# A fused attention and expert kernel: two product evictions made one, the second batch's scores moved by 8 steps, four stores halved

## The chip, the cores and the metric

The kernel runs on one core of a Trainium2 chip. The time is the device time of one execution in microseconds (us); lower is better. The engines are named as in the profile: PE (TensorE's matmuls, PEld its weight loads), DVE (VectorE), ACT (ScalarE), POOL (GpSimd), SP (SyncE). Here POOL and SP mostly issue DMAs.

## What is computed

```
for each of 4 batches (q, k, v: 6080 x 256, float32):
    qn, kn = q, k with each column divided by (its norm over the 6080 rows + 1e-6)
    s  = kn^T @ qn / tau              # 256 x 256, the "scores"
    a  = softmax of s over its last axis
    x  = v @ a                        # 6080 x 256
over all 24320 rows of x:
    h  = x @ w_in                     # 256 -> 2048
    g  = s * relu(h)^2 + b
    out = g @ w_out                   # 2048 -> 256, float32
```

## The kernel before

**Groups and steps.** The 24320 rows are cut into 48 groups (`NG`) of 512 rows; the last has 256. The attention weights of a batch are folded into `w_in` once (`wa`), so that a group needs only `h = v @ wa`. One group has 16 steps (`FT`), one for each 128 of the 2048 hidden columns. Step s belongs to group g = s // 16, and m = s % 16 is its place there. The main loop (L832) writes out the program of every engine in this order, and `po` keeps each engine in program order. In each step stand:

- `mm1` (L641): two matmuls of 512 columns that make one 128-column piece of h in PSUM. The banks of h hold two pieces each, and there are two of them.
- after step 3 of the next group, seven of the `seven_items` of the group before (L808), each a matmul of 128 columns.
- `relu` every second step, on ACT (L651); `square`, partly on ACT (L662), mostly on DVE (L664); `sums_of` on DVE (L735 to L741), which makes S1 to S4.
- what `at_step` put there: loads, scores, norms.

**The seven products.** The second layer of groups 1 to 46 is done as a 2 x 2 block product with seven instead of eight multiplications (Winograd's form). Each product is 16 matmuls. Their order is n = 0 to 6, and after the last matmul of each an eviction follows on DVE by `evacuate` (L669, SCALAR_TENSOR_TENSOR, out = s_out * PSUM + addend):

| n | accumulates in | reads | then |
|---|---|---|---|
| 0 | X | g, w_out | p1: u1 from X and the row constant |
| 1 | Z | S1, T1 | p5: u5 from Z and the row constant |
| 2 | X | S2, T2 | p6: u2 from X and the row constant |
| 3 | Y | g, w_out | p2: output from Y and u1 |
| 4 | X | S3, T3 | p7: output from X and u5 |
| 5 | Z | S4, w_out | p3: output from Z and u2 |
| 6 | X | g, N4 | p4: output from X and the row constant, then the group's store |

X has a PSUM bank of its own, Y and Z are the halves of another; three banks (`ps_o`) go round. X and Z are read and then accumulated further, so the product that follows in the same bank must wait for the eviction: n = 2 for p1, n = 3 for p5 (Y and Z lie in one bank), n = 4 for p6, n = 5 for p2, n = 6 for p7. With seven items to a step, p1 stands in step m = 5, p5 in 7, p6 in 9, p2 in 12, p7 in 14 of the next group; p3 at m = 0 and p4 at m = 2 of the one after. DVE has there, at m = 0, the square of the next group's last pieces, at m = 2 S1, at 3 S2, at 6 S3, at 8 a square, at 10 S4, at 12 a square.

**Stores.** `store` issues one DMA of a group's 512 x 256 outputs on SP (512 KB) after p4. Group 46 stores its first half after p3, and group 47's go through ACT's queue. On SP there are also the crossbar transposes of v (`crossbar_v`, L394), four to a group, issued at m = 6 for the group two later. The output buffers (`opool`) are two.

**Scores of the next batches.** Batch 0's scores come first. Those of batch b are made while the groups of batch b-1 run. The 6080 rows go in 12 chunks of 512 (the last smaller), each in 4 pairs of matmuls into `s_ps` (L148). The plan is the loop of L582: `w0` is the first step of the scores, `w1` the last step before the next batch begins, and the 48 pairs are spread evenly over `span` steps, for the second batch (b = 1) from step 26 to 106. Chunk c's first pair stands at step sc. Its two loads (POOL, `load`, L132: a cast from float32 to float16) stand at sc - 16, the squares of k on ACT (L177) at sc + 3, those of q on DVE (L174) at sc + 6, two folds on DVE (L191) at sc + 9 and sc + 12, and the sum into the first chunk's rows, an accumulating DMA on POOL (L207), at sc + 15. A buffer for a chunk comes from `qk_pool` (8), which also holds the four pieces of `w_out` at the start.

POOL's queue has, besides these, `load_v` (L372): group g's v at step (g-4) * 16 + 2, so groups 3 and 4 at step 2, group 5 at step 18, group 6 at step 34. v has four buffers.

**The beginning.** Group 0's second layer is done plainly (L713), from step 11 to 31, since the seven products' weights aren't ready. DVE and ACT combine and cast those (L509 to L544) in steps 7 to 44. Step 0 begins near 38 us, step 26 at 58.2, step 35 (the first of the seven products) at 65.7.

Of the kernel before, what the change touches and what calls it, by code (L numbers as in the profile page):

```python
# [10 lines left out]
FP32 = mybir.dt.float32  # L11
# [6 lines left out]
def kernel(  # L18
# [13 lines left out]
    P = 128  # L32

    B, N, C = q.shape
# [12 lines left out]
    FT = Dff // P  # L47
    TG = 512
    NG = (NT + TG - 1) // TG
# [6 lines left out]
    def po(ins):  # L56

        tc.keep_in_program_order(ins)
        return ins

    def pool(name, bufs, **kw):
        return ctx.enter_context(tc.tile_pool(name=name, bufs=bufs, **kw))
# [12 lines left out]
    rpool = pool("rpool", 2)  # L75
    gpool = pool("gpool", 2)
    spool = pool("spool", 1)
    upool = pool("upool", 4)
    opool = pool("opool", 2)

    ps_gram = pool("ps_gram", 1, space=PSUM)
# [3 lines left out]
    rowconst = consts.tile([P, C], FP32)  # L85
# [277 lines left out]
    def group(g):  # L363
        t0 = g * TG
        return t0, min(TG, NT - t0) // P
# [183 lines left out]
    def at_step(s, f):  # L549
        side.setdefault(int(s), []).append(f)  # L550
# [3 lines left out]
    first_group = [b * N // TG for b in range(B)]  # L554
# [26 lines left out]
                at_step((g - 2) * FT + 6, lambda g=g: crossbar_v(g))  # L581
    for b in range(1, B):  # L582
        gr = grams[b]
        w0 = first_group[b - 1] * FT + (26 if b == 1 else 6)
        w1 = first_group[b] * FT - 3
        NCH = len(gr.chunks)
        fin_len = 54
        span = (w1 - fin_len) - w0 - 12
        n = NCH * JC
        for c in range(NCH):  # L590
            sc = w0 + span * c * JC / n
            at_step(max(3, sc - 16), lambda gr=gr, c=c: gr.load(c))
            if c == 0:
                at_step(sc, gr.start)
            for j in range(JC):
                at_step(w0 + span * (c * JC + j) / n, lambda gr=gr, c=c, j=j: gr.mm(c, j))

            def norm_step(gr=gr, c=c, sc=sc):
                ops = gr.norm_ops(c)
                for i, f in enumerate(ops):  # L600
                    at_step(int(sc) + 2 + 1 + i * 3, f)
            at_step(sc + 1, norm_step)

        def fin_step(gr=gr, s=w1 - fin_len):
            ops = gr.finish_ops()
            for i, f in enumerate(ops):
                at_step(int(s) + 1 + (FIN[i] if i < len(FIN) else FIN[-1] + 3 * (i - len(FIN) + 1)), f)
        at_step(w1 - fin_len - 12, fin_step)
# [13 lines left out]
    g_tiles, r_tiles, h_tiles, o_sbs, o_plain = {}, {}, {}, {}, {}  # L622
# [43 lines left out]
    def evacuate(dst, src, add, n):  # L666
        if n == 1:
            add = add[:, None, :].broadcast_to((P, 2, add.shape[-1]))
        po(nc.vector.scalar_tensor_tensor(out=dst, in0=src, scalar=s_out, op0=ALU.mult,  # L669
                                          in1=add, op1=ALU.add))  # L670

    def store(g, j0=0, j1=None):
        t0, nj = group(g)
        j1 = nj if j1 is None else j1
        o_sb = o_sbs.pop(g) if j1 == nj else o_sbs[g]
        po((nc.scalar if g == NG - 1 else nc.sync).dma_start(
            out=out[t0 : t0 + nj * P, :].rearrange("(p j) d -> p j d", j=nj)[:, j0:j1, :],
            in_=o_sb[:, j0:j1, :]))
# [43 lines left out]
                    store(g)  # L722


    S = {}

    def sums_of(g, n, i0=0, i1=NP):
# [3 lines left out]
        if i0 == 0:  # L731
            S[n] = spool.tile([P, NP, TG // 2], FP16, tag=f"S{n}", name=f"S{n}")
        T = {k: t[:, i0:i1] for k, t in S.items()}
        if n == 1:
# [8 lines left out]
    def seven_items(g):  # L743
        st = {}
        lo, hi = slice(0, P), slice(P, C)
        G = lambda h, t: lambda: g_tiles[g][:, h, :, ts(t, TG // 2)]
        W = w_out16.rearrange("p (i h) c -> p h i c", h=2)
        U = lambda: upool.tile([P, 2, P], FP32, tag="u", name="u")

        def out_sb(t, half):  # L750
            if g not in o_sbs:
                o_sbs[g] = opool.tile([P, TG // P, C], FP32, tag="o_sb", name="o_sb")
            return o_sbs[g][:, ts(t, 2), half]

        def p1():
            st["u1"] = U()
            evacuate(st["u1"], st["X"], rowconst[:, lo], 1)

        def p5():
            st["u5"] = U()  # L760
            evacuate(st["u5"], st["Z"], rowconst[:, hi], 1)

        def p6():
            st["u2"] = U()
            evacuate(st["u2"], st["X"], rowconst[:, hi], 1)

        def p2():
            evacuate(out_sb(0, lo), st["Y"], st["u1"], 2)

        def p7():  # L770
            evacuate(out_sb(1, hi), st["X"], st["u5"], 2)

        def p3():
            evacuate(out_sb(0, hi), st["Z"], st["u2"], 2)
            if g == NG - 2:
                store(g, 0, 2)

        def p4():
            evacuate(out_sb(1, lo), st["X"], rowconst[:, lo], 1)
            store(g, 2 if g == NG - 2 else 0)  # L780

        def begin(name):
            t = ps_o.tile([P, 2, 2 * P], FP32, tag="o_ps", name="o_ps")
            halves = [t[:, h, :].rearrange("p (j c) -> p j c", j=2) for h in range(2)]
            if name == "X":
                st["X"] = halves[0]
            else:
                st["Z"], st["Y"] = halves

        products = [  # L790
            ("X", G(0, 0), W[:, 0, :, lo], p1),
            ("Z", lambda: S[1], T1, p5),
            ("X", lambda: S[2], T2, p6),
            ("Y", G(1, 0), W[:, 1, :, lo], p2),
            ("X", lambda: S[3], T3, p7),
            ("Z", lambda: S[4], W[:, 1, :, hi], p3),
            ("X", G(1, 1), N4, p4),
        ]
        items = []
        for n, (name, a, w, after) in enumerate(products):  # L800
            for i in range(NP):
                for j in range(2):
                    def f(n=n, name=name, a=a, w=w, after=after, i=i, j=j):
                        first = n < 2 and i == 0 and j == 0
                        if first:
                            begin(name)
                        last = i == NP - 1 and j == 1
                        po(nc.tensor.matmul(st[name][:, j, :], a()[:, i, ts(j, P)], w[:, i, :],  # L808
                                            start=first, stop=last, skip_group_check=True))
                        if last:  # L810
                            after()
                    items.append(f)
        return items
# [18 lines left out]
    for s in range(NS + FT):  # L832
        g, m = divmod(s, FT)
# [3 lines left out]
        if m == SHIFT and 0 < g and g - 1 not in plain:  # L837
            items = seven_items(g - 1)
            work.append((items, 8 if g == NG - 1 else 7))
# [60 lines left out]
```

## Time and profile before

| | us |
|---|---|
| median of 4 runs | 719.30 (719.28 to 719.31) |
| the profiled execution | 719.31 |
| its span, first to last instruction | 717.5 |

The clock granted to the PE over the span is 0.998 of full speed. From the groups of the page, with their mean durations:

| line, engine | what | times | mean ns |
|---|---|---|---|
| L641 PE | first layer, 512 columns | 1408 | 379 |
| L808 PE | seven products, 128 columns | 5152 | 219 |
| L148 PE | scores, 256 columns | 356 | 289 |
| L651 ACT | relu, 1024 elements | 376 | 1022 |
| L664 DVE | square, 2048 elements | 137 | 1219 |
| L735 to L741 DVE | S1 to S4, 2048 elements | 182 | 1216 to 1224 |
| L669 DVE | eviction of 256 columns with u as addend | 138 | 483 |
| L669 DVE | eviction of 256 columns with the row constant | 184 | 479 and 483 |
| L669 DVE | eviction of 512 columns with the row constant (group 0) | 2 | 747 |
| L174 DVE | squares of q, 1024 elements | 39 | 687 |
| L191 DVE | folds, 1024 and 512 elements | 43 and 43 | 687 and 421 |

The durations of matmuls are modelled and overlap, so that of a matmul is longer than the distance to the next. On DVE, too, one instruction begins some 0.09 us before the end of the last as the trace gives it; where nothing is waited for, the distance from start to start is what counts. In the lines of a timeline the columns are the start in us, the duration, engine and line, operation, output and inputs, shapes, how many were merged, and in brackets the engine's idle time before it with what ended it.

### The profile page before, as it was taken

Reading aid. Unit: us, or ns where it says so; the run is one execution under the profiler, and the core shown is the slowest. Engines: PE = TensorE matmul, PEld = TensorE weight load, DVE = VectorE, ACT = ScalarE, POOL = GpSimd, SP = SyncE. Lnnn points to the kernel's source line nnn. Section 1 sums busy time; section 2 is a strip of 40 time slices with the busy share of each in tenths; the row PEclk is TensorE's granted clock in tenths of the full one; section 3 lists DMA queues with packets and bytes.
Section 4 is the critical chain, followed back from the end, with each engine's and each line's share of the span. In section 5 each row is a group of like instructions: output and inputs, shape, how many; then the busy total and the mean of one; then the engine's idle time right before and its main releaser. Section 6 shows DMA issues by size and latency. Waiting matters only on the chain.

```text
span 717.5 us, 17472 instructions
## 1 busy us (share of the span) xinstructions
PE 696.8 (97%) x7419; PEld 503.6 (70%) x7419; DVE 622.4 (87%) x871; ACT 545.5 (76%) x593; POOL 110.2 (15%) x188
## 2 busy tenths in 40 slices
PE   4699999999999999999999999999999999999997
PEld 2556777776677777777677777777668777777777
DVE  4879999988789989998889899998887888888886
ACT  5789877787777777778777778777877777877874
POOL 4532322202102222111010222110000000000000
PEclk9999999999999999999999999999999999999999
DMA  9999999736555978444772877943323323321202
GB/s 236 207 260 168 154 154 161 120 92 124 118 116 109 136 134 144 112 89 94 139 142 55 148 132 126 152 90 83 92 64 74 97 67 75 100 57 51 76 32 74
DMA packets 86606, 83.47 MB, mean 116 GB/s; under 512 B 56224, under 2 KB 61664, under 8 KB 86528
## 3 DMA queue, kind: packets, MB, share of 16 engines
q0 software_dynamic: 26336, 43.40, 38.9%
q1 hardware_dynamic: 59616, 37.64, 22.4%
q8 instruction: 58, 0.95, 0.6%
q10 hardware_dynamic: 576, 1.31, 0.5%
q14 instruction: 20, 0.16, 0.1%
HBM read 78.91 MB, written 24.90 MB: 145 GB/s over the span
## 4 chain that ended last, share of the span: by engine, by line
PE 92%; DMA 4%; DVE 2%; ACT 1%; issue 0%; POOL 0%; DVEq 0%; ACTq 0%
PE h_ps L641 45%; PE o_ps L808 40%; PE s_ps L148 4%; PE wa_ps L321 2%; DMA qk<-in_k_dram 1%; DMA w_in<-in_moe_w_in_dram 1%; DMA raw<-in_q_dram 1%; PE o_ps L713 1%; ACT sq L177 1%; DVE f L191 1%; PE o_ps L687 0%; ACT r L651 0%; DVE sq L174 0%; DVE o_sb L669 0%; POOL w_in L430 0%
## 5 line engine op out<-in xcount | busy, mean ns | idle before, releaser
L651 ACT ACTIVATE r<-h_ps 128x1024 f16<-128x1024 f32 (+1 forms) x384 | 388.2, 1014 | 151.1 <-PE h_ps L641 146.3
L641 PE MATMUL h_ps<-vT,wa 128*128 128x512 f16 (+7 forms) x1632 | 452.0, 364 | 0.1
L808 PEld LDWEIGHTS <-S 128*128 128x128 f16 x2944 | 198.1, 98 | 84.8 <-issue 0.2
L808 PEld LDWEIGHTS <-g 128*128 128x128 f16 x2208 | 155.1, 98 | 74.1
L664 DVE TENSOR_TENSOR g<-r 128x2048 f16<-128x2048 f16 (+2 forms) x150 | 175.0, 1166 | 15.3 <-ACT r L651 14.7
L808 PE MATMUL o_ps<-T,S 128*128 128x128 f16 x2208 | 183.3, 219 | 0.1
L641 PEld LDWEIGHTS <-wa 128*128 128x128 f16 x1632 | 135.9, 98 | 20.6 <-DVE wa L316 0.2
L808 PE MATMUL o_ps<-w_out,g 128*128 128x128 f16 x1472 | 134.2, 219 | 0.2 <-DVE u L669 0.2
L669 DVE SCALAR_TENSOR_TENSOR o_sb<-o_ps,s_out,u 128x256 f32<-128x256 f32 x138 | 66.7, 483 | 50.8 <-PE o_ps L808 48.8
L662 ACT ACTIVATE g<-r 128x1024 f16<-128x1024 f16 (+1 forms) x97 | 100.4, 1035 | 0.2
L148 PE MATMUL s_ps<-qk 128*128 128x256 f16 (+1 forms) x384 | 71.4, 288 | 14.3 <-ACT qk L139 9.0
L372 POOL DMA_DIRECT2D v<-in_v_dram x48 | 31.1, 652 | 266.1 <-DMA vT<-v 208.0
L669 DVE SCALAR_TENSOR_TENSOR u<-o_ps,s_out,rowconst 128x256 f32<-128x256 f32 x138 | 66.1, 479 | 0.0
L808 PE MATMUL o_ps<-w_out,S 128*128 128x128 f16 x736 | 63.5, 219 | 0.0
L808 PE MATMUL o_ps<-N,g 128*128 128x128 f16 x736 | 63.4, 219 | 0.0
L207 POOL DMA_DIRECT2D f<-f x30 | 26.3, 876 | 224.1 <-DVE f L191 181.7
L737 DVE TENSOR_TENSOR S<-S,g 128x2048 f16<-128x2048 f16 (+1 forms) x47 | 56.5, 1201 | 1.3
L177 ACT ACTIVATE sq<-qk 128x1024 f16<-128x1024 f16 (+2 forms) x53 | 54.5, 1041 | 3.9 <-DMA qk<-in_k_dram 2.3
L735 DVE TENSOR_TENSOR S<-g 128x2048 f16<-128x2048 f16 (+1 forms) x47 | 56.1, 1194 | 0.0
L741 DVE TENSOR_TENSOR S<-g,S 128x2048 f16<-128x2048 f16 x46 | 56.0, 1218 | 0.0
L739 DVE TENSOR_TENSOR S<-g 128x2048 f16<-128x2048 f16 x46 | 56.0, 1217 | 0.0
L148 PEld LDWEIGHTS <-qk 128*128 128x128 f16 (+1 forms) x384 | 32.9, 103 | 20.7 <-ACT qk L139 9.5
(76 smaller groups left out, 313.5 us busy)
## 6 DMA issues: line engine op xcount, KB each, us to landing
out_dram<-o_sb SPq DMA_DIRECT2D x46, 512.0 KB, 2.9
v<-in_v_dram POOLq DMA_DIRECT2D x47, 256.0 KB, 4.8
qk<-in_k_dram POOLq DMA_DIRECT2D x42, 256.0 KB, 6.8
qk<-in_q_dram POOLq DMA_DIRECT2D x42, 256.0 KB, 7.6
f<-f POOLq DMA_DIRECT2D x30, 128.0 KB, 3.1
vT<-v SPq DMA_TRANSPOSE x182, 3.1
w<-in_moe_w_out_dram POOLq DMA_DIRECT2D x4, 512.0 KB, 11.1
raw<-in_k_dram SPq DMA_DIRECT2D x2, 512.0 KB, 6.7
```

The costliest lines, as they stand in the source:

```text
L148: po(nc.tensor.matmul(self.s_ps[:, ch, :], qc[:np_, j, ts(ch, P)], kc[:np_, j, :], start=(c == 0 and j == 0 and ch == 0), stop=(c == len(s ...
L177: po(nc.scalar.activation(out=st["sq"][:np_, a, js, :], in_=(qc, kc)[a][:np_, js, :], func=AF.Square))
L641: po(nc.tensor.matmul(dst, wa[:, ci, ts(m, P)], src, start=(ci == 0), stop=(ci == CH - 1), skip_group_check=True))
L651: po(nc.scalar.activation(out=r16[:, :, i % 2, :n], in_=h_tiles.pop((g, i))[:, :, :n], func=AF.Relu))
L662: po(nc.scalar.activation(out=dst, in_=src, func=AF.Square))
L664: po(nc.vector.tensor_mul(dst, src, src))
L669: po(nc.vector.scalar_tensor_tensor(out=dst, in0=src, scalar=s_out, op0=ALU.mult, in1=add, op1=ALU.add))
L735: po(nc.vector.tensor_add(T[1], A21, A22))
L737: po(nc.vector.tensor_sub(T[2], T[1], A11))
L739: po(nc.vector.tensor_sub(T[3], A11, A21))
L741: po(nc.vector.tensor_sub(T[4], A12, T[2]))
L808: po(nc.tensor.matmul(st[name][:, j, :], a()[:, i, ts(j, P)], w[:, i, :], start=first, stop=last, skip_group_check=True))
```

## The change

The change has three parts. First, p2 no longer evicts. Y and Z are laid out interleaved in their bank, so that the bank has the order of the output, and p3 evicts all 512 columns at once; u1 and u2 become halves of one tile, and u5 has a tag of its own. Second, `w0` of the second batch is 34 instead of 26. Third, groups 1 to 4 store in two halves as group 46 does, the first half after p3 and the second after p4.

```diff
-    upool = pool("upool", 4)
+    upool = pool("upool", 2)
...
-        w0 = first_group[b - 1] * FT + (26 if b == 1 else 6)
+        w0 = first_group[b - 1] * FT + (34 if b == 1 else 6)
...
+    HALVES = (1, 2, 3, 4, NG - 2)
...
-        U = lambda: upool.tile([P, 2, P], FP32, tag="u", name="u")
...
         def p1():
-            st["u1"] = U()
-            evacuate(st["u1"], st["X"], rowconst[:, lo], 1)
+            st["u"] = upool.tile([P, 2, C], FP32, tag="u", name="u")
+            evacuate(st["u"][:, :, lo], st["X"], rowconst[:, lo], 1)
 
         def p5():
-            st["u5"] = U()
+            st["u5"] = upool.tile([P, 2, P], FP32, tag="u5", name="u5")
             evacuate(st["u5"], st["Z"], rowconst[:, hi], 1)
 
         def p6():
-            st["u2"] = U()
-            evacuate(st["u2"], st["X"], rowconst[:, hi], 1)
+            evacuate(st["u"][:, :, hi], st["X"], rowconst[:, hi], 1)
 
         def p2():
-            evacuate(out_sb(0, lo), st["Y"], st["u1"], 2)
+            pass
...
         def p3():
-            evacuate(out_sb(0, hi), st["Z"], st["u2"], 2)
-            if g == NG - 2:
+            out_sb(0, lo)
+            evacuate(o_sbs[g][:, 0:2, :], st["YZ"], st["u"], 2)
+            if g in HALVES:
                 store(g, 0, 2)
 
         def p4():
             evacuate(out_sb(1, lo), st["X"], rowconst[:, lo], 1)
-            store(g, 2 if g == NG - 2 else 0)
+            store(g, 2 if g in HALVES else 0)
...
             if name == "X":
                 st["X"] = halves[0]
             else:
-                st["Z"], st["Y"] = halves
+                st["YZ"], st["Y"], st["Z"] = t, t[:, :, lo], t[:, :, hi]
```

## The prediction

> **What bounds the kernel now.** I read the page's busy shares first, then its slices, then the PE's and the VectorE's own lines in order of time around the places that the change touches.
>
> ```profile
> PE 696.8 (97%) x7419; PEld 503.6 (70%) x7419; DVE 622.4 (87%) x871; ACT 545.5 (76%) x593; POOL 110.2 (15%) x188
> PE   4699999999999999999999999999999999999997
> PEclk9999999999999999999999999999999999999999
> ```
>
> The PE is busy from the third slice to the end, at full clock. A step (one pair of first-layer matmuls, seven of the seven products, sometimes two score matmuls) takes 0.82 us, or 1.04 with the score pair: 300.42 to 302.29, for one, is 1.04 and then 0.83. That pace hardly changes between 75 and 700 us, so time can come only from places where the PE stands still. After 58 us I find few. The two that matter lie in steps 39 and 41:
>
> ```profile
> 69.44 0.59 PE L641 MATMUL h_ps<-vT,wa 128*128 128x512 f16 x2
> 69.87 0.80 PE L808 MATMUL o_ps<-T,S 128*128 128x128 f16 x7
> ...
> 70.73 0.59 PE L641 MATMUL h_ps<-vT,wa 128*128 128x512 f16 x2
> ...
> 71.55 0.59 PE L641 MATMUL h_ps<-vT,wa 128*128 128x512 f16 x2
> 71.98 0.61 PE L808 MATMUL o_ps<-T,S 128*128 128x128 f16 x6
> 72.81 0.22 PE L808 MATMUL o_ps<-w_out,g 128*128 128x128 f16 x1 [0.22 <-DVE u L669]
> ```
>
> From 69.44 to 70.73 is 1.29 us where 1.04 is usual; from 71.55 to the next first-layer pair at 73.13 is 1.58. The PE lost 0.25 and 0.54 us to evictions that VectorE made late. The next window shows how near VectorE is to this in group 2:
>
> ```profile
> 79.85 0.48 DVE L669 SCALAR_TENSOR_TENSOR o_sb<-o_ps,s_out,u 128x256 f32<-128x256 f32 x1 [0.53 <-PE o_ps L808]
> 80.25 1.22 DVE L664 TENSOR_TENSOR g<-r 128x2048 f16<-128x2048 f16 x1
> 81.38 0.69 DVE L191 TENSOR_TENSOR f<-sq 128x1024 f16<-128x1024 f16 x1
> 81.98 0.48 DVE L669 SCALAR_TENSOR_TENSOR o_sb<-o_ps,s_out,rowconst 128x256 f32<-128x256 f32 x1
> ...
> 85.71 0.48 DVE L669 SCALAR_TENSOR_TENSOR u<-o_ps,s_out,rowconst 128x256 f32<-128x256 f32 x1
> ```
>
> The p3 eviction at 79.85 waited for the PE; from there VectorE runs without a gap to p1 at 85.71, which ends at 86.19, and the product that needs it (the third of group 2) starts at 86.24. No slack is left there. A start 0.05 us after the eviction's end is the mark of a PE that waited.
>
> **Part 1, one eviction for Y and Z.** It removes p2 (0.48 us) and lengthens p3 from 256 to 512 columns. The 512-column form stands in the trace at L669, twice, mean 747 ns, and the next instruction starts 0.66 us after it; after a 256-column one the next starts 0.40 us later (85.71 to 86.11). So VectorE saves 2 x 0.40 - 0.66 = 0.13 us a group, 6 us over 46 groups, of an engine that isn't the bound: worth nothing by itself. What counts is where the time now stands. In every one of the 46 groups VectorE was idle before p3, waiting for the PE (0.07 to 1.36 us), so p3 can't start earlier, and all behind it moves by 0.66 - 0.40 = 0.26 us, less what idle time stands before p4.
> In the steady groups that gap is 0.22 us, so 0.04 is left, against a slack of 0.37 before S1's product: no cost. Where there's no gap, the 0.26 reaches p1 and p5. I compared, group by group, the end of each eviction and the start of the product that needs it. Group 2: slack 0, so 0.28 lost with the wait of 0.015 already there. Group 3: slack 0, but see part 2. Group 15: p1 ends at 275.49, its product starts at 275.64, 0.10 usable above the 0.05, so 0.16 lost; group 27 the same. Groups 16 and 28: p5 has 0.10 usable and 0.155 arrives, 0.05 each. In the last full group a gap of 0.3 absorbs all but 0.05. Against this the removed p2 frees p7, which held the PE for 0.08 in step 112. Sum: 0.28 + 0.32 + 0.10 + 0.05 - 0.08 = +0.67 us, bounded by 0 below -0.08 (the delay is absorbed everywhere) and by +1.0 (every unslacked group loses the whole 0.26).
> The Trainium skill, VectorE: DVE Perf Modes, section on the TRN2 errata, says that the fixed cost is paid per instruction and advises 512 elements or more: read alone, this speaks for the merge, and by its 120 cycles at 0.96 GHz I estimate 46 x 0.125 = 5.8 us saved, 713.5 in all, if VectorE set the time. The rows show that the PE does, so that sum isn't taken.
>
> **Part 2, the second batch's scores 8 steps later.** The 48 pairs of score matmuls ran in steps 26 to 106, one in 1.69 steps; now from 34 to the same end, one in 1.52. No work goes; loads, L177, L174, L191 and the accumulating DMAs of L207 move with them.
> Gain: steps 26 to 39 lose two L174 (0.60 each), an L191 of 0.60 and one of 0.34, some 2.1 us, from a VectorE that had no gap from 64 to 72. Without them S1 ends near 67.35, its product comes near 67.45, and p1 and p5 are done 0.6 us or more before their products. The 0.25 and the 0.54 go: -0.79.
> Loss: the pairs of steps 26 and 27 cost nothing, since the PE then waited for ACT's backlog (the relu of 58.98 to 60.95); later they cost 2 x 0.22: +0.43. The other pairs cost the same wherever they stand. Net -0.36.
> Density: VectorE's 1.54 us a chunk (0.60 + 0.60 + 0.34) come in 6.08 steps instead of 6.75. Per group that is +0.40 and -0.13 from part 1, on a PE that also takes 0.23 more for its pairs: as full as before. But the places change. Around group 2's p1 stands the same 1.54 us as before, so part 1's number holds. At group 3's p1 one more pair (0.22) gives the PE's side time: 0.06 lost. Behind it, in step 70, an L191 of 0.34 and an L174 of 0.60 now come between S3 and p5, whose usable slack is 0.45: 0.94 - 0.45 = 0.49 lost. Groups 4 to 6 keep their slack. Sum of part 2: -0.36 + 0.55 = +0.19; its bounds are -0.8 (the cover loss hidden too) and +1.0 (all of 0.94 lost, a further one like it).
> POOL: the first chunk's loads were issued at 45.59 and 46.80, ahead of group 5's load of v; now they stand behind it.
>
> ```profile
> 49.26 0.53 POOL L132 DMA_DIRECT2D qk<-in_q_dram  x1 [0.26 <-DMA v<-in_v_dram]
> 58.81 0.53 POOL L372 DMA_DIRECT2D v<-in_v_dram  x1 [9.02 <-DMA vT<-v]
> 59.34 0.54 POOL L132 DMA_DIRECT2D qk<-in_k_dram  x1
> 59.85 0.55 POOL L132 DMA_DIRECT2D qk<-in_q_dram  x1
> ```
>
> That v load waited for group 2's crossbar transposes, the fourth of which landed at 58.26. If it stays at 58.81, the first chunk's q lands as the one issued at 59.85 did, at 65.90, and the PE needs it near 64.83: 1.07 us of waiting. But the transposes were late because the four loads of 45 to 50 lay ahead of them (the first took 8.3 us, later ones 2.3 to 3.2). With these gone the fourth, issued at 53.85, lands near 56.5 and q near 63.9. I take 0 and keep 1.07 for the range. Other loads landed 4.1 to 9.2 us before their use; a tenth more traffic eats part of that, and the last L207 (135.82) has 10 us to the norm sums: 0, at most 1.
>
> **Part 3, halved stores.** Four more issues of 0.33 us on SP, which idles there, each first half 1.7 us earlier. Nothing reads a store but the output buffer's reuse two groups later.
>
> ```profile
> out_dram<-o_sb SPq DMA_DIRECT2D x46, 512.0 KB, 2.9
> out_dram<-o_sb SPq DMA_DIRECT2D x2, 256.0 KB, 2.0
> ```
>
> Two halves in turn take 4.0 against 2.9, 1.1 more, hidden under 14 us of a group; without that cover 4 x 1.1 = 4.4. Value 0. The Trainium skill's DMA: Bandwidth & Descriptors, section Bandwidth, asks for 1 MiB or more a transfer and so speaks against halving; if that reached the path, the 4.4 would make 724.6, and by the row it doesn't.
>
> **Sum.** +0.67 + 0.19 + 0 = +0.86. The profiled execution took 719.31 us (span 717.5 and 1.8 around it), the four runs' median 719.30. 719.31 + 0.86 = 720.2 us.
>
> **Rivals.** *The first chunk comes late* (slower): place step 34, price 1.07 us, from the point where POOL's v load is still issued after 57.7; 719.31 + 0.86 + 1.07 = 721.2. For it: the 9.02 us wait. Against: the transposes' own queue empties. *The relief reaches the PE and nothing is lost behind p3* (faster): -0.79 + 0.43 - 0.08 = -0.44, 718.9; for it VectorE's 0.13 a group, against it the unbroken run from 79.85 to 85.71. *The two parts cancel*, the edits not reaching the PE at all: 719.3. A gain over 1.44 us would need waits that the trace doesn't have: all that I find after 58 us add up to some 1.8.
>
> **Chances.** The forecast 0.60, its own range 719.5 to 720.8; late chunk 0.20; relief 0.12; cancel 0.08. Faster or slower by over 0.2% (1.44 us, about what a measurement of this kernel can tell) means under 717.9 or over 720.7. Slower: most of the late chunk and a seventh of the forecast, 0.27. Faster: two fifths of the relief case at most, 0.05. Within: 0.68. The range leaves out a tenth on each side: 718.7 to 721.5.
>
> **What would show it.** Right: steps 39 and 41 of 1.04 us or less; 512-column L669 of 0.75 us; p1 of group 2 and p5 of group 3 ending 0.05 us before their products; waits of 0.2 there and in groups 15 and 27. Wrong: a score matmul waiting for a load near 65 us, steps of 0.82 and 1.04 throughout (the merge is free), or a store anywhere in the chain of waits.

## The result and the profile after

| | us |
|---|---|
| the changed kernel, median of 41 runs | 720.35 (720.25 to 720.48) |
| the kernel before, median of 61 runs | 719.41 (719.20 to 720.73) |
| ratio | 1.0012, 95% interval 1.0008 to 1.0017 |
| span of the profiled executions | 718.5 after, 717.5 before |

The change costs 0.94 us (0.98 between the two profiled executions, which the account below explains), 0.12 to 0.13%, which is inside the 0.2% that the prediction took as no change, and the forecast was 720.2. The sum came out so well because two errors in it nearly cancel, as the experiments show.

The account used below is made from the order in time of the PE's instructions: for each step, the distance from its first-layer pair to the next step's, less the usual pace (0.82 us, 1.04 with a pair of score matmuls). What is left is time in which the PE waited. The table has the difference between the changed kernel and the one before, for every step from 24 on where it is over 0.04 us. Its sum has 0.01 us from rounding and from smaller differences.

| step | what waits there | predicted | measured |
|---|---|---|---|
| 27 | relu on ACT; the score pairs that filled the wait are gone | +0.43 | +0.43 |
| 39, 41 | p1 and p5 of group 1, which were to be in time | -0.79 | -0.25, -0.13 |
| 37, 45 | S1 and a weight cast, not foreseen | 0 | +0.16, +0.09 |
| 55 | p1 of group 2 | +0.28 | +0.27 |
| 71 | p1 of group 3 | +0.06 | +0.05 |
| 73 | p5 of group 3 | +0.49 | +0.49 |
| 103, 117 | p1 of group 5, S1 of group 6 | 0 | +0.06, +0.07 |
| 112 | p7 of group 5 | -0.08 | -0.08 |
| 263, 455 | p1 of groups 15 and 27 | +0.32 | +0.17, +0.17 |
| 281, 473 | p5 of groups 16 and 28 | +0.10 | +0.05, +0.05 |
| last full group | p1 | +0.05 | 0 |
| the end | from the last landing to the end of the span: 1.53 us before, 0.91 after | 0 | -0.62 |
| sum | | +0.86 | +0.98 |

The page's busy lines after are nearly those of before; VectorE has 6.4 us and 46 instructions less to do, and the time is longer:

```profile
PE 695.9 (97%) x7419; PEld 502.9 (70%) x7419; DVE 616.0 (86%) x825; ACT 545.9 (76%) x593; POOL 110.1 (15%) x188
```

VectorE's order in time around the same place as in the prediction, p3 of group 1 to p1 of group 2:

```profile
79.32 0.75 DVE L669 SCALAR_TENSOR_TENSOR o_sb<-o_ps,s_out,u 128x512 f32<-128x512 f32 x1 [0.41 <-PE o_ps L808]
79.99 1.22 DVE L664 TENSOR_TENSOR g<-r 128x2048 f16<-128x2048 f16 x1
...
84.84 0.68 DVE L174 TENSOR_TENSOR sq<-qk 128x1024 f16<-128x1024 f16 x1
85.44 0.48 DVE L669 SCALAR_TENSOR_TENSOR u<-o_ps,s_out,rowconst 128x256 f32<-128x256 f32 x1
```

p3 still waits for the PE first, the next instruction starts 0.67 us after it instead of 0.40, and p1 starts 6.12 us after p3 where it was 5.86. The PE's seven matmuls of that step, among them the first that needs p1, take 0.84 us instead of 0.55:

```profile
85.47 0.84 PE L808 MATMUL o_ps<-T,S 128*128 128x128 f16 x7
```

At group 3's p5 two norm operations now stand between S3 and the eviction; first VectorE, then the PE:

```profile
102.59 0.42 DVE L191 TENSOR_TENSOR f<-f 128x512 f16<-128x512 f16 x1
102.93 0.69 DVE L174 TENSOR_TENSOR sq<-qk 128x1024 f16<-128x1024 f16 x1
103.53 0.48 DVE L669 SCALAR_TENSOR_TENSOR u<-o_ps,s_out,rowconst 128x256 f32<-128x256 f32 x1
```

```profile
103.24 0.50 PE L808 MATMUL o_ps<-T,S 128*128 128x128 f16 x6
104.06 0.22 PE L808 MATMUL o_ps<-w_out,g 128*128 128x128 f16 x1 [0.33 <-DVE u L669]
```

The eviction ends at 104.01 and its product starts at 104.06, the 0.05 that marks a waiting PE.

In steps 27 and 41 the PE waits for ACT. In step 27 the score pairs no longer fill the wait (the first line). In step 41 the wait for the relu is now the only one (the last line):

```profile
60.11 0.59 PE L641 MATMUL h_ps<-vT,wa 128*128 128x512 f16 x2 [0.33 <-ACT r L651]
...
71.49 0.50 PE L808 MATMUL o_ps<-T,S 128*128 128x128 f16 x6
71.82 0.22 PE L808 MATMUL o_ps<-w_out,g 128*128 128x128 f16 x1
71.88 0.38 PE L148 MATMUL s_ps<-qk 128*128 128x256 f16 x2
72.51 0.59 PE L641 MATMUL h_ps<-vT,wa 128*128 128x512 f16 x2 [0.25 <-ACT r L651]
```

On POOL the v load no longer waits until 58.81, as the prediction argued:

```profile
56.83 0.53 POOL L372 DMA_DIRECT2D v<-in_v_dram  x1 [12.26 <-DMA vT<-v]
57.35 0.54 POOL L132 DMA_DIRECT2D qk<-in_k_dram  x1
57.87 0.55 POOL L132 DMA_DIRECT2D qk<-in_q_dram  x1
```

The fourth transpose landed at 55.92 and the first chunk's q at 63.81, 1.1 us before its matmul at 64.87. So the prediction's readings for this place (56.5, 63.9 and 64.83) held.

### The profile page after: what moved, and what is told of

Same layout as the page of the kernel before. It is cut to its first block, busy times and chain, and to the rows that moved or that the text cites. A ratio compares the mean times of both kernels' runs of the same rounds, so it can differ in the third digit from the quotient of the medians.

```text
span 718.5 us, 17410 instructions
## 1 busy us (share of the span) xinstructions
PE 695.9 (97%) x7419; PEld 502.9 (70%) x7419; DVE 616.0 (86%) x825; ACT 545.9 (76%) x593; POOL 110.1 (15%) x188
## 4 chain that ended last, share of the span: by engine, by line
PE 90%; ACT 3%; DVE 3%; DMA 3%; issue 1%; POOL 0%; DVEq 0%; ACTq 0%; POOLq 0%
PE h_ps L641 44%; PE o_ps L808 39%; PE s_ps L148 4%; PE wa_ps L321 2%; DMA qk<-in_q_dram 1%; DMA raw<-in_q_dram 1%; ACT r L651 1%; DVE f L191 1%; ACT sq L177 1%; ACT g L662 1%; PE o_ps L687 0%; PE o_ps L713 0%; DVE S L738 0%; DVE sq L174 0%; DVE o_sb L669 0%
## 5 line engine op out<-in xcount | busy, mean ns | idle before, releaser
L669 DVE SCALAR_TENSOR_TENSOR o_sb<-o_ps,s_out,u 128x256 f32<-128x256 f32 x92 | 56.8, 617 | 60.6 <-PE o_ps L808 60.6
L148 PE MATMUL s_ps<-qk 128*128 128x256 f16 (+1 forms) x384 | 69.9, 282 | 16.1 <-ACT qk L139 9.3
```

The lines of the kernel that those rows point to most:

```text
L148: po(nc.tensor.matmul(self.s_ps[:, ch, :], qc[:np_, j, ts(ch, P)], kc[:np_, j, :], start=(c == 0 and j == 0 and ch == 0), stop=(c == len(s ...
```

## The experiments

All were timed beside the kernel before on the same chip; the ratio is to that.

### The three parts apart

**e1_merge**: only part 1.

```diff
-        w0 = first_group[b - 1] * FT + (34 if b == 1 else 6)
+        w0 = first_group[b - 1] * FT + (26 if b == 1 else 6)
-    HALVES = (1, 2, 3, 4, NG - 2)
+    HALVES = (NG - 2,)
```

(against the changed kernel)

> Part 1 alone (one eviction for Y and Z; scores from step 26, stores whole). Theory of the later p3: the PE gains waits of about 0.28 us in steps 55 and 71 (p1 of groups 2 and 3), 0.17 us in steps 263 and 455, 0.05 in 281 and 473, and loses the 0.08 of step 112: some 0.9 us more, 720.3 us, unless the end of the program gives some back. Rival, that the eviction saved is free: 719.4 us and no new wait.

720.30 us (before 719.30), ratio 1.0014 (1.0005 to 1.0023). The account has +0.27 in step 55, +0.25 in 71, +0.16 in 263 and in 455, 0.05 in 281 and 473, +0.07 in 117, -0.08 in 112: +0.96 over all steps. The merge alone costs 1.0 us.

**e2_shift**: only part 2, `w0` 34 in the kernel before.

```diff
-        w0 = first_group[b - 1] * FT + (26 if b == 1 else 6)
+        w0 = first_group[b - 1] * FT + (34 if b == 1 else 6)
```

> Part 2 alone (scores from step 34; two evictions, stores whole). Theory: step 27 longer by 0.43 us (the cover lost), step 39 shorter by 0.25, step 41 still waiting 0.4 us for ACT, step 73 longer by 0.49 us (p5 of group 3 behind two norm operations), no wait at 55 and 71, none in 263 and 455: about 0.7 to 0.8 us more, 720.1 us. Rival, that the shift costs only together with the longer p3: 719.4 us or less.

720.05 us, ratio 1.0011 (1.0003 to 1.0020). +0.43 in step 27, -0.25 in 39, -0.10 in 41, +0.09 in 45, +0.12 in 112 (p7 of group 5, not foreseen), no new wait at 55, 71, 263 or 455. Step 73 has +0.28 only, less than expected: without the longer p3, p1 of group 3 begins 0.27 us earlier against the PE's step, and p5 with it. The profiled execution also had a wait of 0.37 in step 34, behind which the 0.16 of step 37 isn't seen:

```profile
65.24 0.39 PE L148 MATMUL s_ps<-qk 128*128 128x256 f16 x2 [0.20 <-DMA qk<-in_q_dram]
```

Here the v load was issued at 57.26 instead of 56.83, and the first chunk's q landed at 65.19, when the PE already waited for it. This execution took 720.28, the median is 720.05. So the rival of the late chunk comes in here by a part of its price, and perhaps not in every execution: in the changed kernel the chunk's margin is 1.1 us. The time of POOL's issue alone doesn't decide it. In e8 below the v load was issued later still, at 57.46, and q landed at 64.27, in time; from its own issue to its landing q took 6.9 us here, 5.9 in the changed kernel and 5.8 in e8.

**e3_stores**: only part 3.

```diff
-            if g == NG - 2:
+            if g in (1, 2, 3, 4, NG - 2):
                 store(g, 0, 2)
...
-            store(g, 2 if g == NG - 2 else 0)
+            store(g, 2 if g in (1, 2, 3, 4, NG - 2) else 0)
```

> Part 3 alone (groups 1 to 4 stored in halves). Theory: nothing waits for a store, 719.4 us, within 0.1. Rival, that smaller transfers cost what the landing times say (4 x 1.1 us) or that they delay the loads beside them: 719.9 us or more, with a wait for a load or a transpose on the PE.

718.67 us (718.55 to 718.87, against 719.19 to 719.48), ratio 0.9991 (0.9982 to 1.0000). A miss of the theory and of its rival: the stores in halves gain 0.63 us. No step of the account differs by over 0.03 us. The last store lands at 715.97, before at 716.00; the span ends at 716.89 instead of 717.53. The gain lies wholly behind the last landing.

**e4_merge_shift**: parts 1 and 2, that is, the changed kernel with `HALVES = (NG - 2,)`.

> Parts 1 and 2 without the halved stores. Theory: 720.35 us, as the changed kernel, with the same waits in steps 27, 37, 41, 55, 73, 263 and 455. Rival, that the halved stores give or take something in company with the other two parts: a difference of 0.2 us or more from the changed kernel.

720.94 us, ratio 1.0023 (1.0014 to 1.0032), with the changed kernel's waits one by one (+1.59 in the account of both). So the rival holds: parts 1 and 2 cost 1.64, and the halved stores give 0.6 back. Alone, the parts come to 1.00 + 0.75 - 0.63 = 1.12 us; the merge and the shift share some of their waits (steps 71, 73 and 112).

### What the halved stores do

The end of SP's program is nine pairs of waits on semaphores and then the end that all engines share. Eight of the pairs hold the eight semaphores of SP's and ACT's DMAs (S101 to S104, then S115 to S118). SP's records of these pairs behind the last landing, with the start in us and the first semaphore of the pair:

```
kernel before     last store signals S104, lands 716.00
  716.02 S104   716.09 S115   716.16 S116   716.55 S117   716.63 S118   span end 717.53
e3_stores         last store signals S118, lands 715.97
  715.99 S118                                                           span end 716.89
changed kernel    last store signals S118, lands 717.58
  717.59 S118                                                           span end 718.49
e6_eight_halves   last store signals S104, lands 716.02
  716.03 S104   716.09 S115   716.16 S116   716.22 S117   716.28 S118   span end 717.18
```

The DMAs of SP and ACT take the eight semaphores in turn, and in all these traces SP waits for them at the end in the same order. Four more DMAs move the last store from the fourth to the eighth in that order, so that the others have been waited for before it lands. Two runs put this to the test.

**e5_late_halves** has (40, 41, 42, 43, NG - 2) in place of e3's groups, **e6_eight_halves** has groups 1 to 8 and NG - 2.

> The kernel before with the stores of groups 40 to 43 halved instead of 1 to 4. Theory of the count: four more hardware DMAs move the last store to the last semaphore that SP waits for at the end, so five waits (0.65 us) are over before it lands: 718.7 us, as with groups 1 to 4. Rival, that earlier stores relieve the crowded start: 719.3 us.

718.73 us (before 719.35), ratio 0.9992 (0.9983 to 1.0000): the same gain late in the kernel, where the page has the DMA engines busy for 1 to 2 tenths (6 to 9 tenths around the stores of groups 1 to 4). It isn't the crowded start.

> The kernel before with the stores of groups 1 to 8 halved: eight more DMAs, the last store on the same semaphore as before. Theory of the count: 719.3 us, the gain gone, with five waits of SP after the last landing. Rival, that halved stores help by themselves: 718.7 us or less.

719.02 us (before 719.35), ratio 0.9995 (0.9986 to 1.0004): half of the gain is gone, not all. No run of it (718.87 to 719.13) is as long as the shortest of the kernel before (719.20). The five waits are back, as the theory has it, but the last of them starts 0.26 us after the landing, not 0.63, because the pause of 0.39 us between S116 and S117 is missing. SP's part of the trace has 342 records before, 350 in e3 and 358 in e6, so the pause may depend on how many instructions stand ahead of it. Its cause is open: the last 8 KB packet of one instruction queue stands at 717.17 us in the trace before, at 712.26 in e3's and at 678.63 in e6's. That could be a load of code that falls elsewhere in a longer program, but at 717.17 the pause is already over, and no run tried it. So of part 3's 0.63 us some 0.3 are the waits themselves, which in e3 are over before the last store lands (shown by e3, e5 and e6), and the rest is the pause, which doesn't stand behind the last landing there either.

### Is it the delay behind p3, or the wide eviction?

**e7_p3_two**: e1 with the bank evicted in two pieces, both at p3.

```diff
-            evacuate(o_sbs[g][:, 0:2, :], st["YZ"], st["u"], 2)
+            for cs in (lo, hi):
+                evacuate(o_sbs[g][:, 0:2, cs], st["YZ"][:, :, cs], st["u"][:, :, cs], 2)
```

> Part 1 alone, but p3 evicts the bank as two evictions of 256 columns: VectorE's work is that of the kernel before, only p2's has moved to p3, and what stands behind p3 is 0.40 us later instead of 0.26. Theory of the later p3: each wait of part 1 alone grows by some 0.13 us (steps 55 and 71 to 0.41, 263 and 455 to 0.30, 281 and 473 to 0.18): 721.1 us. Rival, that the 512-column eviction itself is at fault (its form, its bank): the waits go, 719.3 us.

721.71 us (before 719.35), ratio 1.0032 (1.0020 to 1.0045). The eviction is as before in form and amount and only later, and the cost grows from 1.0 to 2.4 us:

```profile
79.88 0.87 DVE L669 SCALAR_TENSOR_TENSOR o_sb<-o_ps,s_out,u 128x256 f32<-128x256 f32 x2 [0.80 <-PE o_ps L809]
80.67 1.21 DVE L664 TENSOR_TENSOR g<-r 128x2048 f16<-128x2048 f16 x1
```

What follows starts 0.79 us after p3, 0.12 more than with one eviction. The waits of steps 55, 117, 263, 281, 455 and 473 grow by 0.10 to 0.12 each. That of 71 stays, behind a new one of 0.14 in 69. Four others appear or grow, by 0.09 to 0.11 (137, 329, 521, 759). More places than I had counted have less than 0.4 us of slack. The wide form isn't at fault; the place is.

### Order against load

**e8_step71**: the changed kernel with two of VectorE's norm operations one step later.

```diff
+                    late = 1 if gr.b == 1 and (c, i) in ((4, 3), (5, 1)) else 0
-                    at_step(int(sc) + 2 + 1 + i * 3, f)
+                    at_step(int(sc) + 2 + 1 + i * 3 + late, f)
```

> The changed kernel with the second batch's fold of chunk 4 and square of chunk 5 moved from step 70 to 71, behind p5. Theory: the 0.49 us of step 73 go, and most stays gone: 719.9 us. Rival, that VectorE is full there and any order waits as long: the wait turns up in steps 75 to 87 and the time stays at 720.35.

719.91 us (before 719.35), ratio 1.0009 (1.0000 to 1.0018). Step 73's wait is gone (from +0.49 to 0) and comes back nowhere in the profiled execution (719.78). The runs spread more than the others', from 719.64 to 720.77; what the long ones waited for isn't on record.

**e9_act_square**: the changed kernel with chunk 0's square on ACT in step 42 (`late = 5` for `(0, 0)`).

> The changed kernel with ACT's square of the second batch's first chunk (L177) moved from step 37 to 42, out of the run of weight casts. Theory: step 41 waits for ACT because of this square (0.95 us ahead of the relu), so its 0.41 us go, and the 0.10 of step 45 perhaps: 719.9 us. Rival, that the casts alone fill ACT: step 41 still waits 0.4 us, 720.35 us.

720.32 us (before 719.31), ratio 1.0013 (1.0004 to 1.0022). The theory is right for step 41, whose whole 0.54 us of before is gone, and wrong for the time: step 45 now waits 0.45 us for a weight cast that the moved square holds up.

```profile
75.62 0.50 PE L809 MATMUL o_ps<-T,S 128*128 128x128 f16 x6
76.41 0.22 PE L809 MATMUL o_ps<-T,S 128*128 128x128 f16 x1 [0.29 <-ACT T L544]
```

**e10_late_norms**: the kernel before with e3's stores, and of chunks 0 and 1 VectorE's three operations each at steps 40 to 42 and 43 to 45, with three buffers for the squares.

> The kernel before with four halved stores, the scores still from step 26, but VectorE's norm operations of chunks 0 and 1 moved from steps 32 to 44 to steps 40 to 45 (a third buffer for the squares). Theory: the waits of steps 39 and 41 (0.79 us) go without the lost cover of step 27; some comes back behind p6 to p7 of group 1: 718.67 - 0.79 + about 0.3 = 718.2 us. Rival, that VectorE's backlog only moves: 718.7 us.

720.64 us, ratio 1.0017 (1.0008 to 1.0026), 2 us above e3. The waits of 39 and 41 didn't go (-0.06 and +0.07 against before), and steps 46 and 48 each got one of 1.0 us, the first for VectorE's eviction p2, late behind the packed operations. Two theories fell: that the late evictions alone held steps 39 and 41, and that the norm operations could be packed behind them.

**e11_reorder**: the kernel before with e3's stores and seven operations moved, each just behind the eviction that it held up.

```diff
+    MOVED = {(1, 0, 2): 39, (1, 0, 3): 40, (1, 1, 1): 40,
+             (2, 4, 2): 231, (3, 4, 2): 423, (2, 6, 0): 247, (3, 6, 0): 439}
...
-                    at_step(int(sc) + 2 + 1 + i * 3, f)
+                    s = int(sc) + 2 + 1 + i * 3
+                    at_step(MOVED.get((gr.b, c, i), s), f)
```

The keys are the batch, the chunk and the operation (0: k's square on ACT, 1: q's on VectorE, 2 and 3: the folds).

> The kernel before with the halved stores, and seven norm operations put behind the eviction that they held up: of the second batch chunk 0's folds (steps 35 and 38, now 39 and 40) and chunk 1's square on VectorE (38, now 40); of the third and fourth batch a fold of chunk 4 (step m = 6, now 7, behind p5) and ACT's square of chunk 6 (m = 3, now 7). Theory: what stands between an eviction and its product decides, not VectorE's load: the waits of steps 39 and 41 fall by some 0.4 us in all (part comes back in steps 43 to 47), 233 and 425 lose 0.12 each, 249 and 441 lose 0.18 each: 718.67 - 1.0 = 717.7 us. Rival, that the engines are full and the waits only move: 718.7 us.

718.76 us (before 719.31), ratio 0.9991 (0.9982 to 1.0000), no better than e3. The later batches did as expected: steps 233 and 425 lost 0.11 and 0.12, 249 and 441 lost 0.17 each. But 0.67 us came back in steps 44, 46 and 48, and steps 39 and 41 still waited 0.19 and 0.61, although p1 now ended at 69.63 and p5 at 71.16. What held step 41 is in the PE's and VectorE's lines:

```profile
71.85 0.67 PE L811 MATMUL o_ps<-T,S 128*128 128x128 f16 x6
...
73.07 0.59 PE L644 MATMUL h_ps<-vT,wa 128*128 128x512 f16 x2 [0.27 <-ACT r L654]
```

```profile
73.05 1.23 DVE L667 TENSOR_TENSOR g<-r 128x2048 f16<-128x2048 f16 x1 [1.30 <-ACT r L654]
```

VectorE itself sat idle for 1.30 us waiting for ACT. In step 39 the relu of 69.52 ended at 70.55 and the first-layer pair behind it began at 70.60. In both kernels ACT runs without a gap from 66 to 75 us (relus, squares and six weight casts). The trace of the kernel before already has it:

```profile
72.04 1.04 ACT L651 ACTIVATE r<-h_ps 128x1024 f16<-128x1024 f32 x1
```

This relu ended at 73.08, and the first-layer pair of step 42 began at 73.13. Without the relu's end, p5's product (72.81, the line that the prediction shows) and the score pair behind it would have let it begin some 0.04 us sooner. So two engines were late at the same place by about as much, and the profile names only one of them there.

**e12_act_late**: e11 with ACT's square of chunk 1 out of that run as well.

```diff
-    MOVED = {(1, 0, 2): 39, (1, 0, 3): 40, (1, 1, 1): 40,
+    MOVED = {(1, 0, 2): 39, (1, 0, 3): 41, (1, 1, 1): 43,
+             (1, 1, 0): 45, (1, 1, 2): 46, (1, 1, 3): 47,
              (2, 4, 2): 231, (3, 4, 2): 423, (2, 6, 0): 247, (3, 6, 0): 439}
```

> As the reordered kernel, but of the second batch ACT's square of chunk 1 is moved from step 35 to 45, out of the run of weight casts, with that chunk's operations on VectorE behind it (steps 43, 46, 47) and chunk 0's second fold at 41. Theory: in the kernel before, ACT was as late as VectorE in steps 39 to 41 (the casts for the third product and the relu), so both have to be relieved: the waits of 39 and 41 (0.80 us) go, some 0.3 comes back in steps 44 to 48, and the 0.6 us of steps 233, 249, 425 and 441 stay gone: 717.7 us. Rival, that the beginning is full on ACT in any order: the waits turn up in steps 43 to 55, 718.5 us or more.

717.62 us (before 719.39), ratio 0.9976 (0.9966 to 0.9986): better than both kernels, with the scores in their old steps, two evictions for Y and Z, and the halved stores. The whole 0.80 us of steps 39 and 41 is gone, 0.29 comes back in step 55 (not in 44 to 48, as expected), and 0.57 stays gone in the later batches. In step 41 the PE now goes through without a pause:

```profile
71.76 0.50 PE L812 MATMUL o_ps<-T,S 128*128 128x128 f16 x6
72.09 0.22 PE L812 MATMUL o_ps<-w_out,g 128*128 128x128 f16 x1
72.15 0.38 PE L148 MATMUL s_ps<-qk 128*128 128x256 f16 x2
72.37 0.59 PE L645 MATMUL h_ps<-vT,wa 128*128 128x512 f16 x2
```

## Why the prediction was right or wrong

**Part 1 was right in mechanism and nearly in size.** That p3 can't start earlier and what stands behind it moves by 0.26 us is shown by e1 (1.0 us for the merge alone) and by e7, where the delay grew and the cost with it while VectorE's work stayed that of before. The named places are those of the account, to 0.02 us. Alone, the merge costs 1.0 us and not 0.67, mostly because group 3's p1 waits 0.25 there; with the shift, where the prediction counted it, it waits 0.05. Missed were steps 103 and 117 (0.13 us), and the 0.05 of the last group didn't come.
The Trainium skill, VectorE: DVE Perf Modes, section on the TRN2 errata, is borne out for the eviction by itself: one of 512 columns has 751 ns and 0.67 us to the next start, two of 256 have 2 x 0.40. Its advice to make operands of 512 elements or more saved that 0.13 us a group and cost 1.0 us, since the saving fell where VectorE was idle and the added length where it was late.

**Part 2 failed at one step: "The 0.25 and the 0.54 go: -0.79."** Only 0.38 went, and 0.25 came in steps 37 and 45, -0.13 net. The working looked at VectorE alone. There it was right: in the changed kernel p5 of group 1 ends at 70.77, 1.05 us before its product at 71.82. But for steps 39 and 41 it had no row of ACT, though ACT had no gap there either. e11 shows that with VectorE in time the PE waits for ACT, e12 that the 0.80 us go when both are relieved. No run relieved ACT alone in the kernel before; its p5 ended at 72.76 at the end of VectorE's own run without a gap, and its product began at 72.81, so with ACT alone relieved that place would have gained some 0.04 us. The other term was S1: the working had 0.10 us between its end (67.35) and its product, and it ended at 67.58. It reads what the square ahead of it writes, and began 0.03 us after that square's end (65.11 + 1.22, then 66.36), not 0.09 before it. The other two steps held: the lost cover (+0.43) and group 3's p5 (+0.49, taken away by e8).

**Part 3 failed at its value of 0.** "Nothing reads a store but the output buffer's reuse" overlooked the end of the program, where SP waits for the DMA semaphores in an order of its own: -0.63 us (e3). The direction and the order are shown; the cause of the pause, about half of it, stays open. The 1.1 us more of landing time for two halves cost nothing, as said. The Trainium skill's DMA: Bandwidth & Descriptors, section Bandwidth, speaks for larger transfers; here four transfers were halved and the kernel got faster, for a reason that has nothing to do with bandwidth.

The first of these errors made the forecast 0.66 us too fast, the second 0.63 us too slow. That they cancel is luck: the time was met, and two of the three parts were not. Of the rivals, the late chunk didn't come in the changed kernel (its q landed 1.1 us early), and for part of its price in e2 (0.37 us); the relief reached the PE by half, and the merge and the shift didn't leave the PE alone.

## What to carry to other kernels

Where one engine sets the time, what another engine saves is worth what it takes from the waits of the first: look at which instruction waits, what stands just ahead of the eviction it needs, and move the order rather than cut the load. When a wait is named after one engine, ask whether a second is as late there; both have to be relieved. And compare the end of the program behind the last store before a gain of half a microsecond is put down to anything in the middle.

## What the runs showed of the hardware that was not expected

SP's waits at the end of the program start 0.06 to 0.08 us after one another. Between two of them there were 0.36 to 0.39 us in the five kernels with no store halved but group 46's (the kernel before, e1, e2, e4 and e7), and 0.06 in e6, with eight more DMAs; why is open. Four DMAs more in 717 us of work changed the time by 0.63 us (e3), eight more by 0.33 (e6).
